# Shorter lead of a max pass, its first products in another order, and exp products on five banks at the end

## The chip, the cores and the metric

One core of a Trainium2 chip runs the whole program. The metric is the device time of one execution in microseconds (us), the median of several runs.

## What is computed

The input is `x` with 2048 tokens of 512 values, in float32, and a conditioning row `c`. A block of attention and a block of MLP follow each other, each behind a layer normalisation whose scale, shift and gate come from `c`:

```python
mod = (_silu(c) @ w_mod).reshape(c.shape[0], 6, 1, -1)
sa, ca, ga, sb, cb, gb = (mod[:, 0], mod[:, 1], mod[:, 2], mod[:, 3], mod[:, 4], mod[:, 5])
h = _layernorm(x, axis=-1) * (1 + ca) + sa
x = x + ga * _A_ref(h, A_wq, A_wk, A_wv, A_wo)   # 32 heads of 16 queries' values, one head of keys and values, softmax
h = _layernorm(x, axis=-1) * (1 + cb) + sb
x = x + gb * _B_ref(h, B_w1, B_b1, B_w2, B_b2)   # gelu(h @ w1 + b1) @ w2 + b2, 1376 hidden values
```

## The kernel before

**Precision.** Products of weights and activations are made from a high and a low part of each operand (names that end in `H` and `L`), three products instead of one. In the scores, the high and low parts of queries and keys lie in different rows of the same operand (`qst`, `ks`), so that one product with 64 rows does it all. Such a product uses half of the rows of TensorE's array (PE); one on the upper half and one on the lower half can run together. The kernel writes the half as `s` (0 or 1). "Whole" products use all 128 rows.

**Units.** The 2048 queries are cut in 8 blocks of 256, and the 32 heads in 8 groups of 4. A pair of them is a unit; there are 64. For every unit two passes run over all 2048 keys.

- The max pass (`Max.step`, L490 to L529): 32 products `m<-ks,qst` (L505) write 128 x 512 scores each to one of three PSUM banks with the tag "m", and DVE reduces each to its row maximum (L510). After a unit's last reduction, `put_max` takes the maximum over the key blocks (`mm`, L558), transposes it (`turned`, L559), and puts off, by `later`, two steps: `gather` (L553, four copies on POOL, then the split in `mh` and `ml`), and `send` (L548, four DMAs that write the maxima into rows 48 and 49 of the unit's `qst`). `MAX_WAIT` holds by how many clocks each is put off.
- The exp pass (`sexp`, from L588): 8 steps of 4 products `e<-qst,ks` (L607), whose rows 48 and 49 subtract the maximum in the same product. ACT makes the exponential of each (L611). The results `p` go into 16 small products with the values, `acc` (L628, `pv`). The `e` products use three banks in turn (`banks`).

A unit's exp pass cannot start before its maxima have landed in `qst`.

**The order.** Each engine works through its list in the order in which the program writes the instructions; no scheduler changes it. The main loop (from L1349) goes through the units in double steps, steps X and Y. A double step has 8 products of `e`, 32 of `acc`, normally 8 products of the max pass of a later unit, and one batch of other products from a queue. `lead` says how far the max pass is ahead: `LEAD` = 6 means 24 products more than the next unit needs. `clock` counts 4 in a double step; `later(n, fn)` has `fn` done n clocks on, when `due()` comes by.

**The queue.** It holds the query projections of later blocks, and for each block, once its attention is done, `rest`: the output projection (`wops`), the second normalisation (`ve`, `rs`, `xh`, on POOL for most blocks), the transposes (`tp`), the first layer of the MLP (`w1ps`) with its gelu, and the second (`w2ps`). `take` gives out a batch of such products, cut by `batches`. In the loop they are issued as halves (`halves`), so that they share the array with products of the scores. `rest` of block b runs beside the attention of block b + 1. What is left of block 6's `w2` products after the loop fills pauses in the tail, where block 7's `rest` runs alone (`tick`, `TAIL`), as whole products.

**The prologue.** `SLOTS` lists in what order key, value and query projections, transposes and other preparations are written, and how many products of the max pass (`chunk`) go between. `FIRST_MAX` is the order of the first products, of units 0 and 1, by key blocks of 512: unit 0 block 0, unit 1 block 0, and so on. Each (unit, block) is 8 products by (twice 4). `low_k` (L400, on DVE) makes the low half of a key block, and `repeat_k` (L404, on ACT) copies it to the other half of the array. `keep_warm(WARM[3])` (L1348) issues five products without use ahead of the first `e`.

**Two lines at the change.** `modl` (L290) are products for the second normalisation's scale and shift, which are put in the prologue by `late_rows`; `qL` is the low part of a query projection, which `send_q` writes to memory (`dq`), from where `load_q` fetches it to `qst`.

Of the kernel before, what the change touches and what calls it, by code (L numbers as in the profile page):

```python
# [18 lines left out]

GELU_R = 0.044715 ** 0.5  # L20

LEAD = 6
LEAD_0 = 6
FIRST_MAX = ((0, 0), (1, 0), (0, 1), (1, 1), (0, 2), (0, 3), (1, 2), (1, 3))
SLOTS = ((2, "keys 1", "keys 1"), (2, "keys 1", "keys 1"), (2, "low 1", "heads 2"), (2, "heads 2", "k 1"), (1, "warm"), (1, "heads 2"), (2, "heads 2", "v 0"),
# [4 lines left out]
MAX_WAIT = (1, 4)  # L30
QBUFS = 4
PREP = 4
BUSY = 5
# [3 lines left out]
TAIL = (4, 8)  # L37
GROUP = 4
NORM_WAIT = 6
WARM = (4, 16, 2, 5)  # L40
MOD_WAIT = 3
AHEAD = 4.5
STIR = ((0, 4, 8, 12), (16, 32, 48, 0))
# [2 lines left out]
def raw(ap):  # L46
    return ap.bitcast(F32)
# [3 lines left out]
def adaln_mqa_mlp(  # L51
# [99 lines left out]
    def due():  # L151
        now = [p for p in pending if p[0] <= clock[0]]
        pending[:] = [p for p in pending if p[0] > clock[0]]
        for _, fn in now:
            fn()
# [11 lines left out]
    def batches(ps, pairs, size, ready=lambda n: True, begin=True, end=True):  # L167

        todo = [(a, b_) for wh, wl, xh, xl in pairs for a, b_ in ((wh, xh), (wl, xh), (wh, xl))]
        last = len(todo) - 1  # L170

        ends = list(range(len(todo), 0, -size))[::-1]
        for begin_, end_ in zip([0] + ends, ends):
            part = range(begin_, end_)
            while not ready(part[-1] // 3):
                yield -1
            yield [(ps, *todo[n], begin and n == 0, end and n == last) for n in part]
# [255 lines left out]
    def qproj(b, g):  # L433

        ps = psum.tile([P, BQ], F32, name=f"qps{b}_{g}", tag="v" if g else "x")
        yield from mm3(ps, qpairs(b, g), 3, 1)
        qH, qL = qtiles(b, g)
        if g == 0:
            nc.scalar.copy(qH, ps)
            nc.vector.tensor_tensor(out=qL, in0=ps, in1=raw(qH), op=ALU.subtract)  # L440
        else:
            q32 = pro.tile([P, BQ], F32, name=f"q32_{b}_{g}", tag="h32", bufs=4)
            nc.scalar.copy(q32, ps)
            split(qH, qL, q32, act, pool)
        send_q(b, g, qH, qL)
        yield -2

# [32 lines left out]
    class Max:  # L480


        def __init__(self):
            def products(u, kcs):
                return [(u, j, t, kc) for kc in kcs for j in range(2) for t in range(blocks[units[u][0]][1] // P)]

            def in_rows(u):
                return [(u, j, t, kc) for j in range(2) for t in range(blocks[units[u][0]][1] // P) for kc in range(NKC)]


            begin = [o for u, kc in FIRST_MAX for o in products(u, [kc])]
            self.todo = [begin + [o for u in range(2, NU) for o in in_rows(u)] for _ in range(2)]
            self.mx, self.left, self.done = {}, list(size), 0

# [34 lines left out]
    def put_max(u, mx):  # L529

        T = blocks[units[u][0]][1] // P
        qst = qsts[u]
        mm = mms[u % 2]
        turned = att.tile([P, 32], F32, name=f"turned{u}", tag="turned", bufs=2)
        if u == 0:
            pad(att, 256, "pad7")
        mt = att.tile([4 * T, P], F32, name=f"mt{u}", tag="mt", bufs=2)
        mh = att.tile([4 * T, P], F32R, name=f"mh{u}", tag="mh", bufs=2)  # L540
        ml = att.tile([4 * T, P], F32R, name=f"ml{u}", tag="ml", bufs=2)

        def send():
            for s in range(2):
                for r, src in ((48, mh), (49, ml)):
                    dst = qst[64 * s + r:64 * s + r + 1].rearrange("p j (t n) -> p (j t) n", n=P)
                    ring = nc.scalar if u == 0 and s else nc.sync
                    ring.dma_start(out=raw(dst), in_=raw(src[2 * T * s:2 * T * (s + 1), :].unsqueeze(1)))  # L548
            placed.add(u)

        def gather():
            for g in range(0, P, 32):
                nc.gpsimd.tensor_scalar(out=mt[:, g:g + 32], in0=turned[g:g + 4 * T, :], scalar1=1.0, scalar2=0.0,  # L553
                                        op0=ALU.mult, op1=ALU.add)
            split(mh, ml, mt, nc.gpsimd, nc.gpsimd)

        def reduce():
            nc.vector.tensor_reduce(out=mm[:, :4 * T], in_=mx, axis=AX.X, op=ALU.max)  # L558
            nc.vector.transpose(out=turned, in_=mm)  # L559
            later(MAX_WAIT[0], gather)  # L560
            later(MAX_WAIT[1], send)


        if NQ <= u < NQ + 2:
            reduce()
        else:
            later((0 - clock[0]) % 4 + 1, reduce)
# [22 lines left out]
    def sexp(u, K, j, s, line=None):  # L590

        w = blocks[units[u][0]][1]
        qst = qsts[u]
        assert u in placed
        n = u * steps[0] + K
        if n < 3 and n not in pbufs:
            pbufs[n] = att.tile([P, 2, 2, 512], F32, name=f"p{n}", tag="p", bufs=3)
        pt = pbufs[n % 3]
        bank = banks.pop(0)
        banks.append(bank)  # L600
        e = psum.tile([P, 512], F32, name=f"e{u}_{K}_{j}_{s}", tag=f"e{bank}", bufs=1)
        rows = slice(64 * s, 64 * s + 64)
        if w == 512:
            kt, rhs = K, qst[rows, j, :]
        else:
            kt, rhs = 2 * K + j, qst[rows].rearrange("p j n -> p (j n)")
        nc.tensor.matmul(e, ks[rows, kt * P:(kt + 1) * P], rhs, start=True, stop=True)  # L607
        dst = pt[:, j, s, :]

        def exp():  # L610
            ins = nc.scalar.activation(dst, e, AF.Exp, scale=0.25)  # L611
            for old in written.pop((n - 3, j, s), ()):
                tc.declare_no_dep(ins.ins, old, reason="the products that read the tile's last contents come between the two")
            written.setdefault((n, j, s), []).append(ins.ins.name)
            return ins

        return exp() if line is None else line.append(exp)
# [190 lines left out]
    def rest_steps(b, fast, rp, bank, ons, ready):  # L808
# [4 lines left out]
        for hf in range(w // HQ):  # L813
# [201 lines left out]
            for t in range(2):  # L1015
                sl = slice(t * P, (t + 1) * P)
                for cols in (slice(0, D), ):
                    place = dict(tag="m", bufs=3) if b == len(blocks) - 2 and t else bank()
                    ps = psum.tile([P, D], F32, name=f"w2ps{b}_{hf}_{t}_{cols.start}", **place)
                    ops = [(gH[:, f, sl], gL[:, f, sl], w2H[:, f, cols], w2L[:, f, cols]) for f in range(NF)]  # L1020
                    size_ = BATCH - 1 if b == len(blocks) - 2 and not t else BATCH
                    yield from batches(ps[:, :cols.stop - cols.start], ops, size_, lambda f: made.issuperset(range(f + 1)))
                    if fast:
                        later(1, lambda t=t, ps=ps, cols=cols: store(t, ps, cols))
                        yield 2
                    else:
                        store(t, ps)
# [126 lines left out]
    def resume():  # L1154

        go_on(holder[0])
# [69 lines left out]
    def q_group():  # L1226
        for i in range(KD):
            next(projections[0])
            if i == KD - 1:
                next(projections.pop(0))  # L1230
            yield

    def warm():
        keep_warm(WARM[2], tag="x")
# [112 lines left out]

    keep_warm(WARM[3], tag="e2", bufs=1)  # L1348
    behind = None  # L1349
    for u in range(NU):  # L1350
        for K in range(0, steps[u], 2):
            goal = lead[u] + (lead[u + 1] - lead[u]) * (K + 2) / steps[u]
# [37 lines left out]

            due()
            batch = take() if behind else None
            short = batch and products(batch) < SHORT + 0.01
            if short:
                issue(mixture(maxes(1, n // 2), exps(1, [(X, 0), (X, 1)])),
                      exps(0, [(X, 0)]) + halves(batch, 0) + [(1.0, lambda: follow(0, X, 1))])
            elif batch:
                groups = [mixture(maxes(1, n // 2, 0.01), beside(1, [(X, 0), (X, 1), (Y, 0)])),  # L1400
                          halves(batch, 0) + [(1.0, lambda: follow(0, X, 0))]]
                issue(*(reversed(groups) if batch[0][3] else groups))
            else:
                plain(1, X, 0, (n + 2) // 4)
# [3 lines left out]
                end_step(*behind)  # L1408
            clock[0] += 1
            due()  # L1410
            if batch:

                reduces, gone = [], []

# [85 lines left out]
```

## Time and profile before

| | |
|---|---|
| median of 3 runs | 1564.13 us |
| the runs | 1564.13, 1564.03, 1564.39 us |
| span of the profiled execution | 1563.1 us, clock 1.000 |
| PE busy | 1546.5 us (99%) |
| DVE busy | 1401.7 us (90%) |
| ACT busy | 1228.8 us (79%) |
| POOL busy | 681.7 us (44%) |

The profiled execution gives its span only, from its first to its last instruction; the timed runs lie about 1 us above it. Rows of the profile name the line, the engine, the operation and output<-input; "x" gives how many. In a row of the timeline the first two numbers are the start and the duration in us, and a bracket at its end says how long the engine was idle before and who ended that. PEld is PE's weight load.

### The profile page before, as it was taken

What the parts mean: (1) busy time and instruction counts of PE and PEld (TensorE: products, weight loads), DVE (VectorE), ACT (ScalarE), POOL (GpSimd) and SP (SyncE); (2) the same over time, 40 slices, a digit from 0 to 9 for tenths busy, and PEclk for the clock granted to TensorE, in tenths of its full rate; (3) what the DMA queues carried; (4) which work ended last, traced back from release to release, by engine and by line L of the source; (5) the groups of instructions that cost most, each with busy time, mean ns of one, the idle gap of its engine ahead of it and who ended that gap; (6) DMA issues with size and microseconds to landing.
All of it is one profiled execution on the core that took longest, in us unless ns stands there. A gap on an engine that the chain in (4) does not pass through costs nothing.

```text
span 1563.1 us, 41433 instructions
## 1 busy us (share of the span) xinstructions
PE 1546.5 (99%) x16387; PEld 959.9 (61%) x16387; DVE 1401.7 (90%) x2479; ACT 1228.8 (79%) x2392; POOL 681.7 (44%) x1194
## 2 busy tenths in 40 slices
PE   7999999999999999999999999999999999999999
PEld 4455555567655665557655675556655676556667
DVE  7999999999999999999999999999999999999625
ACT  5577778788777887788877887788877888788853
POOL 5545433877323570246422472245611573235711
PEclk9999999999999999999999999999999999999999
DMA  7235412313030211213022120303112130312241
GB/s 244 97 96 194 152 52 89 120 52 97 19 110 19 83 60 35 93 29 99 29 62 69 57 84 26 105 16 97 43 50 79 46 97 20 102 34 66 81 150 61
DMA packets 83126, 121.63 MB, mean 78 GB/s; under 512 B 19614, under 2 KB 56222, under 8 KB 82676
## 3 DMA queue, kind: packets, MB, share of 16 engines
q1 hardware_dynamic: 82916, 118.97, 23.5%
q8 instruction: 130, 2.13, 0.6%
q14 instruction: 64, 0.52, 0.1%
q10 hardware_dynamic: 16, 0.00, 0.0%
HBM read 91.13 MB, written 27.27 MB: 76 GB/s over the span
## 4 chain that ended last, share of the span: by engine, by line
PE 84%; DVE 10%; issue 3%; POOL 2%; DMA 1%; ACT 0%; ACTq 0%; SPq 0%; POOLq 0%; DVEq 0%
PE acc L628 28%; PE m L505 24%; PE e L607 16%; DVE mx L510 8%; PE w1ps L191 8%; PE w2ps L181 2%; PE w2ps L191 1%; PE w1ps L181 1%; DMA xt<-in_A_x_dram 1%; PE qps L191 1%; PE tp L191 1%; PE wops L191 1%; PE kps L162 1%; DVE st L835 1%; DVE x L828 1%
## 5 line engine op out<-in xcount | busy, mean ns | idle before, releaser
L510 DVE TENSOR_REDUCE mx<-m 128x1 f32<-128x512 f32 x2048 | 1270.5, 682 | 86.9 <-PE m L505 63.8
L611 ACT ACTIVATE p<-e 128x512 f32<-128x512 f32 x2048 | 1099.3, 598 | 257.4 <-PE e L607 110.5
L505 PE MATMUL m<-ks,qst 64*128 64x512 f32 x2048 | 832.4, 429 | 1.9 <-DVE mx L510 0.6
L607 PE MATMUL e<-qst,ks 64*128 64x512 f32 x2048 | 747.6, 412 | 0.1
L628 PE MATMUL acc<-p,va 128*32 128x256 f32 x8192 | 548.0, 385 | 0.0
L505 PEld LDWEIGHTS m<-ks,qst 64*128 64x128 f32 x2048 | 366.5, 184 | 212.3 <-DVE mx L510 174.8
L607 PEld LDWEIGHTS e<-qst,ks 64*128 64x128 f32 x2048 | 362.5, 184 | 95.2 <-ACT p L611 71.1
L628 PEld LDWEIGHTS acc<-p,va 128*32 128x32 f32 x8192 | 213.7, 109 | 213.1 <-issue 110.0
L553 POOL TENSOR_SCALAR mt<-turned 8x32 f32<-8x32 f32 x256 | 53.1, 208 | 418.9 <-DVE turned L559 406.9
L191 PE MATMUL w1ps<-h2H,w1t 64*128 64x256 f32 x1232 | 235.6, 287 | 0.0
L191 PEld LDWEIGHTS w1ps<-h2H,w1t 64*128 64x128 f32 x1232 | 185.8, 184 | 28.9 <-DVE mx L510 17.7
L191 PE MATMUL w1ps<-h2L,w1t 64*128 64x256 f32 x616 | 169.2, 275 | 0.0
L191 PE MATMUL w2ps<-w2H,gH 64*128 64x512 f32 x284 | 123.8, 436 | 0.0
L191 PEld LDWEIGHTS w1ps<-h2L,w1t 64*128 64x128 f32 x616 | 114.0, 185 | 0.0
L191 PE MATMUL w2ps<-w2L,gH 64*128 64x512 f32 x282 | 110.9, 393 | 0.0
L191 PE MATMUL w2ps<-w2H,gL 64*128 64x512 f32 x282 | 110.2, 391 | 0.0
L954 POOL TENSOR_SCALAR tt<-tt 128x256 f32<-128x256 f32 x77 | 31.0, 403 | 142.6 <-ACT tt L953 109.3
L137 POOL TENSOR_TENSOR gL<-z,gH 128x256 fp32r<-128x256 f32 x77 | 57.0, 740 | 6.4
L955 POOL TENSOR_TENSOR tt<-tt,z 128x256 f32<-128x256 f32 x77 | 56.7, 736 | 6.4
L965 POOL TENSOR_TENSOR z<-tt,z 128x256 f32<-128x256 f32 x77 | 56.4, 733 | 6.0
L964 POOL TENSOR_TENSOR tt<-tt,z 128x256 f32<-128x256 f32 x77 | 56.4, 732 | 0.0
L191 PEld LDWEIGHTS w2ps<-w2H,gL 64*128 64x128 f32 x282 | 52.2, 185 | 0.4
(190 smaller groups left out, 1480.9 us busy)
## 6 DMA issues: line engine op xcount, KB each, us to landing
w1t<-dw SPq DMA_DIRECT2D x82, 512.0 KB
qst<-dq SPq DMA_DIRECT2D x384, 32.0 KB
do<-oc SPq DMA_DIRECT2D x64, 128.0 KB
dw<-w1s SPq DMA_DIRECT2D x11, 512.0 KB
xt<-in_A_x_dram SPq DMA_DIRECT2D x4, 1024.0 KB
dq<-qH SPq DMA_DIRECT2D x16, 256.0 KB
dq<-qL SPq DMA_DIRECT2D x16, 256.0 KB
x<-in_A_x_dram SPq DMA_DIRECT2D x8, 512.0 KB
```

What stands on the lines that cost most here:

```text
L137: eng_l.tensor_tensor(out=dst_l, in0=src, in1=raw(dst_h), op=ALU.subtract)
L181: nc.tensor.matmul(ps, a, b_, start=first_, stop=last_)
L191: ins = nc.tensor.matmul(ps, a[rows], b_[rows], start=first_ and s == 0, stop=last_ and s == 1)
L505: nc.tensor.matmul(m, qsts[u][rows, j, t * P:(t + 1) * P], ks[rows, kc * 512:(kc + 1) * 512], start=True, stop=True)
L510: nc.vector.tensor_reduce(out=self.mx[u][:, i, kc:kc + 1], in_=m, axis=AX.X, op=ALU.max)
L553: nc.gpsimd.tensor_scalar(out=mt[:, g:g + 32], in0=turned[g:g + 4 * T, :], scalar1=1.0, scalar2=0.0, op0=ALU.mult, op1=ALU.add)
L607: nc.tensor.matmul(e, ks[rows, kt * P:(kt + 1) * P], rhs, start=True, stop=True)
L611: ins = nc.scalar.activation(dst, e, AF.Exp, scale=0.25)
L628: ins = nc.tensor.matmul(accs[u][32 * cidx:32 * cidx + 32, :], va[:, kt, :], rhs, start=kt == 0, stop=kt == NKT - 1)
L955: nc.gpsimd.tensor_tensor(out=tt, in0=tt, in1=z, op=ALU.mult)
L964: nc.gpsimd.tensor_tensor(out=tt, in0=tt, in1=z, op=ALU.mult)
L965: nc.gpsimd.tensor_tensor(out=z, in0=tt, in1=z, op=ALU.add)
```

## The change

1. The lead of the max pass falls from 24 to 16 products (`LEAD`, `LEAD_0`). In PE's list in the loop, each max product is one that came a double step earlier in the order of the max pass, and the max pass ends one double step later: 12 instead of 14 steps have none.
2. `FIRST_MAX` puts four products of unit 1's second key block behind unit 0's third and fourth block; unit 0 is complete after 44 products, not 48. `SLOTS` is rearranged: `v 2`, `q 1` and `v 3` come earlier, `rows` (the `modl` products) comes last and behind unit 0's end.
3. In the prologue's query projection, the subtraction for `qL` comes after a pause of its generator, and with it the sends. In `gather` of unit 0, two of the four copies are on ACT.
4. The five products without use ahead of the first `e` go (`WARM`).
5. `send` comes two clocks after the maximum instead of four (`MAX_WAIT`).
6. When no max products are left, two of the banks with the tag "m" join the three of the `e` products. Each step then writes its four `e` products first, alternating between the halves, then half of a batch of `w2` products as whole ones.
7. Block 6's first `w2` tile takes batches of 4 (`SHORT`) instead of 5, and `batches` lets a leading batch of one product join the next. 25 instead of 28 `w2` products of block 6 are done in the loop; the tail has 17 instead of 20 in front of the last `wops` and 24 instead of 18 behind it.

By the lists of the engines, POOL's copies for the units whose number is 3 mod 8 (from 11 on) come behind `ve` and `rs` of the block and ahead of `xh`. The five-bank part and the constants, from the diff:

```diff
-LEAD = 6
-LEAD_0 = 6
-FIRST_MAX = ((0, 0), (1, 0), (0, 1), (1, 1), (0, 2), (0, 3), (1, 2), (1, 3))
+LEAD = 4
+LEAD_0 = 4
+FIRST_MAX = ((0, 0, 4), (1, 0, 4), (0, 1, 4), (1, 1, 2), (0, 2, 4), (0, 3, 4), (1, 1, 2), (1, 2, 4), (1, 3, 4))
...
-         (0, "v 2"), (2, "q 1"), (2, "q 1"), (2, "q 1"),
-         (2, "q 1", "rows"), (2, "v 3", "wq 2"), (2, "rows"), (2, "rows"), (2, "rows", "wq 3", "load"))
-MAX_WAIT = (1, 4)
+         (0, "v 2", "q 1"), (2, "q 1"), (2, "q 1"), (2, "q 1"), (2, "q 1", "v 3"),
+         (2, "rows", "wq 2"), (2, "rows"), (0, "rows"), (0, "rows", "wq 3", "load"))
+MAX_WAIT = (1, 2)
...
-WARM = (4, 16, 2, 5)
+WARM = (4, 16, 2, 0)
...
         ends = list(range(len(todo), 0, -size))[::-1]
+        if ends[0] == 1:
+            ends.pop(0)
...
-            split(qH, qL, q32, act, pool)
+            nc.scalar.copy(qH, q32)
+            yield -2
+            nc.gpsimd.tensor_tensor(out=qL, in0=q32, in1=raw(qH), op=ALU.subtract)
...
-            begin = [o for u, kc in FIRST_MAX for o in products(u, [kc])]
+            parts = {(u, kc): products(u, [kc]) for u in range(2) for kc in range(NKC)}
+            begin = [parts[u, kc].pop(0) for u, kc, n in FIRST_MAX for _ in range(n)]
...
+                if u == 0 and g >= P // 2:
+                    nc.scalar.copy(mt[:, g:g + 32], turned[g:g + 4 * T, :])
+                    continue
...
-        e = psum.tile([P, 512], F32, name=f"e{u}_{K}_{j}_{s}", tag=f"e{bank}", bufs=1)
+        if not isinstance(bank, int):
+            e = bank
+        else:
+            e = psum.tile([P, 512], F32, name=f"e{u}_{K}_{j}_{s}", tag=f"e{bank}", bufs=1)
...
-                    size_ = BATCH - 1 if b == len(blocks) - 2 and not t else BATCH
+                    size_ = SHORT if b == len(blocks) - 2 and not t else BATCH
...
+            if not bare[0] and not mp.has(0) and not mp.has(1):
+                bare[0] = True
+                banks[:0] = [psum.tile([P, 512], F32, name=f"e_{i}", tag="m", bufs=3) for i in range(2)]
+
+            def alone(K, part):
+                issue(exps(0, [(K, 0), (K, 1)]), exps(1, [(K, 0), (K, 1)]))
+                whole(part)
+
             due()
             batch = take() if behind else None
             short = batch and products(batch) < SHORT + 0.01
-            if short:
+            if bare[0]:
+                alone(X, batch[:len(batch) // 2] if batch else [])
+            elif short:
...
-            if batch:
+            if bare[0]:
+                alone(Y, batch[len(batch) // 2:] if batch else [])
+                if batch:
+                    resume()
+                    advance()
+            elif batch:
```

More of the change, by code (lines that the diff above doesn't have):

```diff
@@ L488, in in_rows @@
                 return [(u, j, t, kc) for j in range(2) for t in range(blocks[units[u][0]][1] // P) for kc in range(NKC)]
-            begin = [o for u, kc in FIRST_MAX for o in products(u, [kc])]
+            parts = {(u, kc): products(u, [kc]) for u in range(2) for kc in range(NKC)}
+            begin = [parts[u, kc].pop(0) for u, kc, n in FIRST_MAX for _ in range(n)]
+            assert not any(parts.values())
             self.todo = [begin + [o for u in range(2, NU) for o in in_rows(u)] for _ in range(2)]
@@ L1229, in q_group @@
             if i == KD - 1:
-                next(projections.pop(0))
+                last = projections.pop(0)
+                next(last)
             yield
+        next(last, None)
+        yield
     def warm():
@@ L1349, in adaln_mqa_mlp @@
     behind = None
+    bare = [False]
     for u in range(NU):
```

## The prediction, made before the changed kernel ran

> **What bounds the kernel now.** I read the page first: the span, the engines' shares, the chain that ended last and the costliest groups.
>
> ```profile
> span 1563.1 us, 41433 instructions
> PE 1546.5 (99%) x16387; PEld 959.9 (61%) x16387; DVE 1401.7 (90%) x2479; ACT 1228.8 (79%) x2392; POOL 681.7 (44%) x1194
> PE 84%; DVE 10%; issue 3%; POOL 2%; DMA 1%; ACT 0%; ACTq 0%; SPq 0%; POOLq 0%; DVEq 0%
> L510 DVE TENSOR_REDUCE mx<-m 128x1 f32<-128x512 f32 x2048 | 1270.5, 682 | 86.9 <-PE m L505 63.8
> ...
> L607 PE MATMUL e<-qst,ks 64*128 64x512 f32 x2048 | 747.6, 412 | 0.1
> ```
>
> PE is busy 99% of the span and holds 84% of the chain. DVE, with its 2048 reductions of the max pass, comes next. In front of its 2048 exp products PE lost 0.1 us in all (last column): every unit's maxima were in place in time. The profiled execution's span is 1563.1 us; the timed runs (median 1564.13) lie 1.0 above it, and I add that 1.0 to every sum. Then the windows, by stage: one block of the main loop, and the stretch near its end in which no max products are left.
>
> ```profile
> 297.00:477.00 180.00, 179.90 (x2017) 112.50 (x2012) 168.67 (x295) 147.49 (x289) 88.61 (x153) 1.00 0.22 67
> 1478.00:1510.00 32.00, 32.00 (x312) 18.17 (x311) 1.76 (x2) 26.76 (x52) 10.93 (x19) 1.00 0.24 84
> ```
>
> The columns are the window, its length, then busy time of PE, PE's weight loads, DVE, ACT and POOL, the granted clock (1.00), and the DMA share. In a block PE works 179.90 of 180.00 us. So from the first exp product to the end of the loop every us that goes must be a us of PE work, and every wait that is added in front of a PE instruction is paid whole. Only three places are not like this: the prologue, the stretch without max products, and the tail. The change touches all three. As written out per engine, PE's list inside the loop stays the same, except that each max product there is one that came eight places (one double step) earlier in the max pass's order.
>
> **The prologue: about 1.5 us earlier.** The loop's first exp products wait for unit 0's maximum. The chain of waits and the engines' timeline:
>
> ```profile
> 71.61 0.93 ACTq L548
> ...
> 72.63 2.18 DMA qst<-ml
> ...
> 74.85 0.56 PE e L607 x2
> ```
>
> ```profile
> 53.64 0.68 DVE L400 TENSOR_TENSOR ks<-kps,ks 16x512 fp32r<-16x512 f32 x1
> 54.35 0.62 ACT L404 CAST ks<-ks 16x512 fp32r<-16x512 f32 x1 [0.75 <-DVE ks L400]
> 59.66 0.68 DVE L400 TENSOR_TENSOR ks<-kps,ks 16x512 fp32r<-16x512 f32 x1
> 60.38 5.22 DVE L510 TENSOR_REDUCE mx<-m 128x1 f32<-128x512 f32 x8
> 66.63 2.48 DVE L510 TENSOR_REDUCE mx<-m 128x1 f32<-128x512 f32 x4 [1.03 <-PE m L505]
> 69.67 1.02 POOL L553 TENSOR_SCALAR mt<-turned 8x32 f32<-8x32 f32 x4 [0.33 <-DVE turned L559]
> 73.35 1.42 PE L285 MATMUL idle<-wkH 128*128 128x512 f32 x5
> ```
>
> Unit 0's maximum ends with the reduction that is over at 69.11 (66.63 + 2.48), the 48th. The new order puts four products of unit 1's second key block behind it, so it is the 44th: 4 x 0.65 (5.22 / 8) = 2.6 us less. Against it stands that DVE no longer has those reductions to do while a key block's low half is made and copied. In the old list the subtraction at 53.64 was followed by reductions that need nothing new; now unit 0's products of block 2 come at once, and they need the copy of 54.35 (to 54.97) and a product before DVE can go on. A reduction could begin at about 55.5 (54.97 and a product of 0.5), where one began at 54.35: 1.1 lost. At block 3 (59.66) the pattern is the same, but the products moved behind block 2 cover about half of it: 0.5, an estimate. So 2.6 - 1.6 = 1.0. The gather of the maxima, four copies of 0.26 on POOL, now has two on ACT: 0.5. The five idle products that go (1.42 us at 73.35) ended before the rows landed at 74.81, so they cost nothing now. The first exp product then starts at about 73.3 instead of 74.85. Bounds: 0 if the waits eat all of it; 3.1 (2.6 + 0.5) if there are none. The value is nearer the middle, -1.5.
>
> **The steps without max products: about -3.3 us.** These are the starts of the accumulation (`acc`) in the chain of waits; one step lies between two of them.
>
> ```profile
> 1468.44 1.00 PE acc L628 x16
> ...
> 1471.28 1.00 PE acc L628 x16
> ...
> 1474.08 1.00 PE acc L628 x16
> ...
> 1476.88 1.00 PE acc L628 x16
> ...
> 1508.32 1.86 PE acc L628 x32
> ```
>
> A step with max products takes 2.84 (1471.28 - 1468.44); the two without them that still have `w1` halves take 2.80; the twelve with `w2` halves take 31.44 / 12 = 2.62. PE's list after the change has max products in the former two (2 x 0.04 = +0.1) and the new form in all twelve: four exp products alternating between the array's halves, then two (once three) whole `w2` products, then `acc`. What such groups cost is seen where half and whole products follow each other in the prologue:
>
> ```profile
> 62.45 0.50 PE L505 MATMUL m<-ks,qst 64*128 64x512 f32 x2
> 62.87 0.50 PE L162 MATMUL qps<-h0H,wqH 128*128 128x512 f32 x1
> 63.22 0.39 PE L162 MATMUL qps<-h0H,wqL 128*128 128x512 f32 x1
> 63.45 0.40 PE L162 MATMUL qps<-h0L,wqH 128*128 128x512 f32 x1
> 63.77 0.50 PE L505 MATMUL m<-ks,qst 64*128 64x512 f32 x2
> ```
>
> A pair of halves to the first whole product is 0.42, the next starts are 0.35 and 0.23 apart, and 0.32 goes to the next pair: a group of k takes 0.23 k + 0.2. So a new step is 1.00 (`acc`) + (2 x 0.23 + 0.2) + (2 x 0.23 + 0.2) = 2.32, against 2.62: 12 x 0.30 = 3.6, less 0.23 for the third product, 3.3. ACT does not take over: four exps in a row take 2.06 (next row), 1.96 from start to start, under 2.32; with three banks it stands idle 0.3 a step, with five it need not.
>
> ```profile
> 1478.35 2.06 ACT L611 ACTIVATE p<-e 128x512 f32<-128x512 f32 x4
> ```
>
> That the exp products pair up is as good as shown: the two `m` halves at 62.45 took one slot and the change (0.42), not two slots. Bounds: 0 if waits for banks eat the difference; -5.9 if changing between halves and whole costs nothing (2.12 a step).
>
> **The tail: +1.4 us.** The shorter batches leave more of block 6's `w2` products for behind the loop: 17 instead of 20 in front of the last `wops`, 24 instead of 18 behind it.
>
> ```profile
> 1514.55 4.59 PE w2ps L181 x20
> 1519.14 1.89 PE wops L181 x6
> 1521.04 4.13 PE w2ps L181 x18
> 1525.17 0.44 PE tp L912 x4
> ```
>
> ```profile
> 1518.68 0.41 ACT L132 CAST onH<-os_last 128x256 fp32r<-128x256 f32 x1 [8.05 <-DVE os_last L666]
> 1525.02 0.55 DVE L847 TENSOR_SCALAR xh<-x,mv,rs 128x512 f32<-128x512 f32 x1 [0.46 <-POOL rs L844]
> ```
>
> The last `wops` starts at 1519.14 because `onH` is cast until 1519.09, so three products fewer ahead of it leave PE idle and gain nothing. Behind it the transposes `tp` started as the filling ended, with the normalised rows nearly there; six more products are 6 x 0.229 (4.13 / 18) = +1.4 on the path.
>
> **The shorter lead: 0 as I take it.** Each unit's maximum is now ready one double step (5.6 us) less ahead of its first exp product. Where nothing stands in between, the sends come two clocks, half a double step (2.8), earlier behind the gather than before, so those units lose only the other half, and I take it that each of them had that much in hand, since none was late before (0.1 us). The tight ones are the seven whose number is 3 mod 8 (11 to 59): POOL's copies for them now stand behind the normalisation's two small operations, and the sends wait for that.
>
> ```profile
> 672.61 0.24 POOL L842 TENSOR_SCALAR ve<-mv 128x2 f32<-128x2 f32 x1 [4.41 <-DVE mv L841]
> 672.93 0.72 POOL L844 TENSOR_TENSOR rs<-ve,mhalf 128x2 f32<-128x2 f32 x1
> 673.76 4.14 POOL L847 TENSOR_SCALAR xh<-x,mv,rs 128x512 f32<-128x512 f32 x2
> 678.97 0.29 PEld L607 LDWEIGHTS e<-qst,ks 64*128 64x128 f32 x2
> ```
>
> ```profile
> 1469.91 0.33 SPq L646 DMA_DIRECT2D do<-oc  x1
> 1471.60 0.58 SPq L705 DMA_DIRECT2D sums<-do  x1
> ```
>
> In unit 27 `rs` ends at 673.65. Four copies, the cast and the subtraction as in unit 0 (1.02 + 0.06 + 0.3 + 0.5) and four issues bring the last issue to about 677.2; the exp product needs the row at 678.97, 1.77 later. The nearest rows are 1.69 (on SP's queue, from the issue of `do` at 1469.91 to its reader at 1471.60) and 2.18 (unit 0's `ml`, on ACT's queue). These sends are on SP's queue, so I take 1.69: in time, 0. At 2.18 each is 0.41 late, 7 x 0.41 = +2.9. `xh` itself moves behind the copies by 1.9 us, to the moment at which the transposes need it: 0. Unit 63's copies now stand behind the last gelu operations; being one unit, it is small beside the seven.
>
> [...]
>
> **Sum.** -1.5 - 3.3 + 0.1 + 1.4 + 0 = -3.3: a span of 1559.8, a time of 1560.8 us.
>
> **Rivals.** First, *the rows come late* (slower). Same place, the seven units above: if the last issue and the landing together pass the 1.77 us by a stall s, the time is 1560.8 + 7 s. It decides at s = 0.92, a landing of 2.7 us, and beyond that cancels and outruns the gain: s = 0.92 gives 1567.3, s = 1.1 gives 1568.5. For it: SP's line also carries the weight loads, and behind these a send can wait; no slack remains to take it. Against: the same queue shows 1.69. With the 2.18 of the other queue it is 1563.7, no change. Second, *the new steps gain nothing* (2.62 stays, because four exp products in a row meet banks that ACT has not emptied yet, or because the changes between halves and whole cost more than in the prologue): 1560.8 + 3.3 = 1564.1, no change. Against: ACT's 1.96. Third, *the prologue gains nothing*, the waits for the key blocks take the place of the four reductions: 1562.3, no change by itself. Fourth, *more gain*: no loss in changing between halves and whole, 2.12 a step, 1558.2. For it: within a group the products already start 0.23 apart. Against: the 0.42 and 0.35 above.
>
> **How the numbers follow.** 0.2% (3.1 us) is about what a measurement of this kernel can tell from no change, so faster starts below 1561.0, and my forecast lies just beyond that line. Chances: the forecast, give or take 1.2, 0.50, of which 0.33 is below the line; more gain 0.13; late rows 0.22, of which 0.15 is far enough to be slower; no gain in the steps or the prologue 0.15, which is no change. Faster 0.46, same 0.17 + 0.07 + 0.15 = 0.39, slower 0.15. The range reaches down to 1557.4 (more gain, and half of what the prologue may still give), up to 1565.6 (neither gain, with the +1.5 of tail and steps left); outside lie the late rows that make it slower, 0.15, and 0.05 below.
>
> **What would show it.** Right: the first exp product near 73.3; `acc` of the last twelve steps 2.3 apart, with ACT nearly without idle time; the last transposes about 1.4 later behind the end of the loop; in blocks, 180 us as before. Wrong: exp products whose idle time ends with the rows `qst<-ml` in units 11 to 59; `acc` starts 2.6 apart; a first exp product at 74.8.

## The result: slower by 0.6%, and the profile after

The changed kernel takes 1573.50 us (median of 5 runs, 1571.87 to 1575.34) against 1564.14 us before (5 runs, 1564.03 to 1565.55): the ratio is 1.0057, with a 95% interval of 1.0046 to 1.0068. The forecast was 1560.8 us, with a range up to 1565.6. PE's granted clock, as a share of full speed, is 1.000 in the trace of the kernel before; beside the experiments that kernel was timed 60 times more, at 0.999 or 1.000 in all but four (0.997 and 0.998, 1567.1 to 1568.5 us). The changed kernel's runs have 0.994 to 0.998, and the longer ones have the lower clocks on the whole.

From the page of the changed kernel (span; busy time; exp products with PE's idle time in front of them in the last column):

```profile
span 1570.3 us, 41358 instructions
PE 1546.9 (99%) x16354; PEld 957.0 (61%) x16354; DVE 1400.9 (89%) x2479; ACT 1229.7 (78%) x2394; POOL 681.2 (43%) x1192
L619 PE MATMUL e<-qst,ks 64*128 64x512 f32 x2048 | 742.7, 412 | 5.4 <-DMA qst<-ml 5.4
```

PE waits 5.4 us for the rows of maxima, where it waited 0.1. Where, tells the list of waits, over the whole span and from 297 to 480 us alone (us in total, times, longest):

```profile
PE e L619 <- DMA qst<-ml: 5.4, 3, 4.2
...
PE e L619 <- DMA qst<-ml: 4.5, 2, 4.2
```

Most of it is one wait of 4.2 us, at unit 12. The clock shows in the windows; it changes at 64.56, 67.98, 344.46 and 351.28, the ends of the rows with 0.50 (window, length, busy time of PE, PE's weight loads, DVE, ACT, POOL, then the clock, 0.50 for half speed):

```profile
57.74:61.15 3.41, 3.41 (x16) 1.69 (x15) 3.33 (x6) 1.56 (x3) 0.00 (x0) 1.00 0.02 5
61.15:64.56 3.41, 2.36 (x9) 1.10 (x8) 2.16 (x4) 1.01 (x3) 0.00 (x0) 1.00 0.00 0
64.56:67.98 3.42, 3.42 (x10) 1.84 (x8) 2.40 (x4) 0.00 (x0) 0.00 (x0) 0.50 0.00 0
...
341.04:344.46 3.42, 1.64 (x20) 0.60 (x18) 2.43 (x5) 1.36 (x4) 2.98 (x9) 1.00 0.01 3
344.46:351.28 6.82, 4.41 (x34) 3.26 (x34) 2.08 (x3) 2.28 (x4) 0.27 (x1) 0.50 0.13 33
```

Twice PE worked at half clock: for 3.4 us in the prologue, behind a window in which it was busy 2.36 of 3.41 us, and for 6.8 us at unit 12, behind one with 1.64 of 3.42. In the second stretch PE worked 4.41 us at half speed, so it lost about 2.2, an estimate (4.41 / 2). In the kernel before, the window of this length around the same place of the prologue held 3.13 us of PE work:

```profile
59.12:62.53 3.41, 3.13 (x11) 1.52 (x11) 3.29 (x6) 1.34 (x3) 0.00 (x0) 1.00 0.00 0
```

PE's list holds the exp products in the same order in both kernels, so their starts can be compared one by one. Read from the two timelines:

| | before | after | later by | added since the row above |
|---|---|---|---|---|
| first of unit 0 | 74.85 | 75.23 | 0.38 | 0.38 |
| first of unit 12 | 341.22 | 346.88 | 5.66 | 5.28: the wait (4.34) and 0.94 in units 9 to 11 |
| first of unit 13 | 364.02 | 371.85 | 7.83 | 2.17: half clock |
| first of unit 59 | 1399.17 | 1408.35 | 9.18 | 1.35: 0.3 at a time |
| start of the last `acc` | 1508.32 | 1514.46 | 6.14 | -3.04: the steps without max products |
| end of the span | 1563.1 | 1570.3 | 7.2 | 1.06: the tail |

The steps at the end did what was forecast. In the chain of waits:

```profile
1486.14 1.00 PE acc L640 x16
...
1488.53 1.00 PE acc L640 x16
...
1512.14 1.00 PE acc L640 x16
...
1514.46 1.88 PE acc L640 x32
...
1520.71 3.91 PE w2ps L183 x17
...
1524.64 1.89 PE wops L183 x6
1526.53 5.51 PE w2ps L183 x24
1532.04 0.44 PE tp L924 x4
```

From 1486.14 to 1514.46 there are twelve steps, 28.32 us, 2.36 each.

Why unit 12 waits is seen on POOL's and SP's timelines. Its maxima are turned on DVE, then copied by POOL (`mt`), then sent:

```profile
334.49 0.21 DVE L568 STREAM_TRANSPOSE turned<-mm 128x32 f32<-128x32 f32 x1
334.97 1.28 POOL L1144 TENSOR_TENSOR w2f<-w2f,gb 128x512 f32<-128x512 f32 x1
...
338.29 1.29 POOL L1144 TENSOR_TENSOR w2f<-w2f,gb 128x512 f32<-128x512 f32 x1
...
341.63 1.02 POOL L562 TENSOR_SCALAR mt<-turned 8x32 f32<-8x32 f32 x4
...
345.10 0.57 SPq L554 DMA_DIRECT2D qst<-ml  x1
...
346.88 0.76 PE L619 MATMUL e<-qst,ks 64*128 64x512 f32 x1 [4.20 <-DMA qst<-ml]
```

And before:

```profile
327.74 0.21 DVE L559 STREAM_TRANSPOSE turned<-mm 128x32 f32<-128x32 f32 x1
...
328.23 1.02 POOL L553 TENSOR_SCALAR mt<-turned 8x32 f32<-8x32 f32 x4
...
333.80 1.28 POOL L1132 TENSOR_TENSOR w2f<-w2f,gb 128x512 f32<-128x512 f32 x1
```

The last two pieces of `w2`, scaled and split on POOL (334.97 to 341.67 after), stood behind unit 12's copies before; with the shorter lead they stand ahead of them. `turned` is ready at 334.70 and waits 6.9 us.

### The profile page after: what moved, and what is told of

Same layout as the page of the kernel before. It is cut to its first block, busy times and chain, and to the rows that moved or that the text cites. A ratio compares the mean times of both kernels' runs of the same rounds, so it can differ in the third digit from the quotient of the medians.

```text
span 1570.3 us, 41358 instructions
## 1 busy us (share of the span) xinstructions
PE 1546.9 (99%) x16354; PEld 957.0 (61%) x16354; DVE 1400.9 (89%) x2479; ACT 1229.7 (78%) x2394; POOL 681.2 (43%) x1192
## 4 chain that ended last, share of the span: by engine, by line
PE 91%; DVE 5%; DMA 1%; POOL 1%; ACT 1%; issue 0%; SPq 0%; DVEq 0%; POOLq 0%
PE acc L640 31%; PE m L511 26%; PE e L619 17%; PE w1ps L193 8%; DVE mx L516 4%; PE w2ps L183 2%; PE w2ps L193 2%; PE qps L193 1%; PE wops L193 1%; PE w1ps L183 1%; DMA xt<-in_A_x_dram 1%; PE tp L193 1%; PE kps L162 1%; PE wops L183 0%; DMA qst<-ml 0%; PE tp L375 0%
## 5 line engine op out<-in xcount | busy, mean ns | idle before, releaser
L193 PE MATMUL w2ps<-w2H,gH 64*128 64x512 f32 x264 | 115.8, 439 | 0.0
L193 PE MATMUL w2ps<-w2L,gH 64*128 64x512 f32 x264 | 103.5, 392 | 0.0
L193 PE MATMUL w2ps<-w2H,gL 64*128 64x512 f32 x264 | 103.0, 390 | 0.0
L976 POOL TENSOR_TENSOR tt<-tt,z 128x256 f32<-128x256 f32 x77 | 56.5, 733 | 0.0
```

The lines of the kernel that those rows point to most:

```text
L193: ins = nc.tensor.matmul(ps, a[rows], b_[rows], start=first_ and s == 0, stop=last_ and s == 1)
L976: nc.gpsimd.tensor_tensor(out=tt, in0=tt, in1=z, op=ALU.mult)
```

## The experiments

Theory 1: the loss is one place on POOL's list, and the pauses of PE that it and the new prologue make bring the clock to half. Theory 2: the rows land late through SP's line or the DMAs. Theory 3: the loss is spread over the units.

**The weight pieces put aside.** In the changed kernel, no weights are prepared while unit 11 runs.

```diff
-            if clock[0] >= prepared[0] + PREP and weights and weights[0] in preps and not state["busy"]:
+            if clock[0] >= prepared[0] + PREP and weights and weights[0] in preps and not state["busy"] and u != 11:
```

> The changed kernel, but the last two pieces of w2 are not prepared while unit 11 runs, so POOL has the gather of unit 12 ahead of them in its list. Theory 1 (the loss is one place: unit 12's copies stand behind 6.7 us of weight preparation on POOL, its first exp product waits 4.2 us, and in that pause the clock gate falls to half for 6.8 us): the wait of unit 12 goes, and 4.2 + about 2.2 us with it, against the changed kernel's 1573.5: 1566 to 1567.5, and the mean clock rises to 0.999 (one half-speed stretch of 3.4 us in the prologue left). Theory 2 (the rows land late because SP's line or the DMAs are slow, wherever POOL has the copies): unit 12 is as late as before, 1572 to 1575.

Measured: 1571.95 us (1570.64 to 1576.73), ratio to before 1.0053 (1.0041 to 1.0066). Unit 12's rows were in time, so theory 2 falls; the time did not follow. The two pieces now stand between the steps of the gelu on POOL, and ACT waits for these with its exponentials queued behind:

```profile
350.88 1.28 POOL L1144 TENSOR_TENSOR w2f<-w2f,gb 128x512 f32<-128x512 f32 x1
...
354.96 0.72 POOL L977 TENSOR_TENSOR z<-tt,z 128x256 f32<-128x256 f32 x1
355.72 0.42 ACT L965 ACTIVATE tt<-z 128x256 f32<-128x256 f32 x1 [4.05 <-POOL z L977]
...
356.67 0.79 PE L619 MATMUL e<-qst,ks 64*128 64x512 f32 x1 [3.51 <-ACT p L623]
```

A wait of 3.5 us for a free bank took the place of the 4.2, and behind it the clock was at half for 6.8 us again (355.51 to 362.34; 16 `acc` products took 1.94 us at 357.40, 1.07 at 350.49): 6.3 us are lost between the first products of units 12 and 13, where the changed kernel loses 6.5 around unit 12. In this run the prologue kept its full clock, and the first exp product came at 73.28.

**Unit 12's wait filled.**

```diff
+            if (u, K) == (12, 0):
+                ps = psum.tile([P, 512], F32, name="fill12", tag=f"e{banks[0]}", bufs=1)
+                for _ in range(18):
+                    nc.tensor.matmul(ps, ks[:, 0:P], ks[:, 0:512], start=True, stop=True)
```

> The changed kernel with 18 products without use (18 x 0.23 = 4.1 us) put in PE's list in front of unit 12's first exp product, so that PE works through the wait; nothing is done to the wait itself. If the clock falls because PE is idle (theory 1), it stays at 1 there: first exp product of unit 12 at the same 346.9, but 2.2 us less behind it: 1570 to 1572. If the clock falls for another reason (the load of the chip, the phase of something free-running), nothing changes: 1572 to 1575.

Measured: 1577.14 us (1571.66 to 1578.22), ratio 1.0071 (1.0058 to 1.0083). The median is worse than that of the changed kernel; in the profiled run (clock 0.995) the prologue, which is unchanged, had 17 us at half clock (first exp product at 79.53), and the runs' clocks go from 0.992 to 1.000. So the time decides nothing here. At unit 12, where the test is, the windows show full clock, through the filled wait (first row) and behind it:

```profile
347.64:351.05 3.41, 3.41 (x17) 2.58 (x15) 0.00 (x0) 0.00 (x0) 1.38 (x3) 1.00 0.01 2
351.05:354.46 3.41, 3.41 (x42) 2.44 (x42) 2.49 (x5) 2.52 (x6) 0.00 (x0) 1.00 0.14 41
```

Unit 12 is 4.3 us later again, and between units 12 and 16 only 0.15 more is lost, where it was 2.1. So in this trace the half clock there went when PE no longer stood idle, with the wait itself still in place.

**The prologue filled, first try.**

```diff
+            "fill 2": one(lambda: keep_warm(3, tag="e0", bufs=1)), "fill 3": one(lambda: keep_warm(3, tag="e1", bufs=1)),
```

(`fill 2` stands behind the first `keys 3` in `SLOTS`, `fill 3` behind the first `q 1`.)

> The changed kernel with three products without use ahead of unit 0's first product on key block 2, and three ahead of that on block 3, where PE waits 0.9 us each for the keys' low half. If these pauses bring the clock down to half at 64.6 us (for 3.4 us), it stays at 1 now, DVE gets its products sooner, and the first exp product comes 1.0 to 1.7 us earlier than 75.2; the time falls by as much, to about 1572. If the clock has another cause, the first exp product stays at 75.2 or comes a little later, and the time is that of the changed kernel.

Measured: 1580.32 us (1575.52 to 1581.73), ratio 1.0092 (1.0079 to 1.0105). The bank was one that ACT still had to read, so the filling itself waited, and the pause grew to 1.78 us. Timeline, then windows:

```profile
56.44 0.97 PE L287 MATMUL idle<-wkH 128*128 128x512 f32 x3 [1.78 <-ACT va L415]
```

```profile
54.85:58.26 3.41, 1.82 (x7) 1.12 (x8) 1.04 (x2) 1.55 (x4) 1.50 (x3) 1.00 0.00 0
58.26:82.15 23.89, 23.05 (x66) 10.30 (x68) 13.46 (x23) 4.77 (x12) 2.57 (x7) 0.50 0.02 7
```

Behind the longer pause came a longer stretch at half clock, 23.9 us, and the five runs, at clocks of 0.990 to 0.997, are all slower than those of the changed kernel. Against its intention, this speaks for the pauses. That the pause alone sets the length is not shown: the run before this one had 17 us with the pauses of the changed kernel.

**The same on a free bank** (both with `tag="e2"`).

> As the filled prologue before it (three products without use ahead of unit 0's products on key blocks 2 and 3), but written to a PSUM bank that nothing holds, so that they don't wait themselves: in the first try they waited for a copy out of their bank and made the pause longer (1.78 us), and the clock was at half for 23.9 us. If pauses of PE bring the clock down, now no stretch of half speed should be left before the first exp product in any run: it comes at 73.0 to 73.6, the loss of unit 12 (4.3 and 1.6 to 2.2) stays, and the time is 1570 to 1572 with a spread of under 2 us. If pauses don't matter, the prologue's half-speed stretches come and go as before, and the runs spread by 4 us and more.

Measured: 1571.97 us (1570.73 to 1572.48), ratio 1.0046 (1.0034 to 1.0058), spread 1.8 us. No half clock ahead of the loop; the windows that were short of work are now 3.07 busy:

```profile
53.57:56.98 3.41, 3.07 (x11) 1.54 (x9) 2.65 (x5) 2.22 (x6) 1.48 (x2) 1.00 0.00 0
60.40:63.81 3.41, 3.07 (x12) 1.83 (x11) 2.74 (x5) 1.93 (x4) 0.00 (x0) 1.00 0.02 5
```

The first exp product comes at 73.94, not the 73.0 to 73.6 expected, 0.7 to 1.0 us later than in the two traces that kept full clock without the filling (72.98 and 73.28). What is left over the kernel before is unit 12 and the small losses.

**The lead back in the loop alone** (`LEAD = 6`, `LEAD_0 = 4`).

> The changed kernel with LEAD = 6 again (LEAD_0 stays 4, so the prologue is the same and the lead grows by 8 products over units 0 to 7). Theory 1: from unit 8 on the gather of unit 12 has its old place ahead of the weight preparation, so the wait goes with its half-speed stretch (-6.4), and with it the small losses of 0.3 in front of the units 3 mod 8 (-1.9); against it 8 more products in the first eight units, which cost DVE or PE up to 1: 1564.5 to 1566.5. Theory 3 (the loss is spread over all units by the new steps and sends): under 2 us of it goes, 1571 or more.

Measured: 1569.77 us (1566.75 to 1576.18), ratio 1.0037 (1.0022 to 1.0052); higher than expected. In the profiled run (1566.75, clock 1.000) unit 12's copies are at 332.14, ahead of both weight pieces, as before, and PE waits for rows 0.2 us in all:

```profile
332.14 1.01 POOL L562 TENSOR_SCALAR mt<-turned 8x32 f32<-8x32 f32 x4
337.73 1.28 POOL L1144 TENSOR_TENSOR w2f<-w2f,gb 128x512 f32<-128x512 f32 x1
```

```profile
PE e L619 <- DMA qst<-ml: 0.2, 1, 0.2
```

From unit 12 to unit 56 it loses nothing against the kernel before. But making up the eight products over units 0 to 7 costs 5.8 us (from 1.9 earlier at unit 0 to 3.9 later at unit 12), not 1. The other runs, up to 1576, have clocks of 0.993 to 0.999; where the clock fell in them no trace shows.

**Unit 12's copies on ACT and DVE.**

```diff
+        def gather12():
+            for g in range(0, P, 32):
+                nc.scalar.copy(mt[:, g:g + 32], turned[g:g + 4 * T, :])
+            split(mh, ml, mt, nc.scalar, nc.vector)
...
-            later(MAX_WAIT[0], gather)
+            later(MAX_WAIT[0], gather12 if u == 12 else gather)
```

> The changed kernel, but unit 12's maxima are copied by ACT (four copies and the high part) and DVE (the low part), not by POOL; nothing else is moved, and the weight preparation stays where it is on POOL. If POOL's line is what makes unit 12 late, its wait of 4.3 us and the half-speed stretch behind it go, and nothing comes in their place: 6 us less than the changed kernel, span 1562 to 1564 where the prologue keeps full clock, mean clock 0.998 to 1.0. If SP or the landing is to blame, the wait stays at 3 us or more.

Measured: 1570.46 us (1568.57 to 1573.77), ratio 1.0044 (1.0031 to 1.0057). Unit 12's last rows are sent 7.6 us ahead of its first exp product (339.82 and 347.38), and PE no longer waits for them, with POOL's weights where they were. In place of that wait DVE, with the low part in its line, waits for ACT 1.4 us, and PE then for DVE:

```profile
337.82 0.28 DVE L137 TENSOR_TENSOR ml<-mt,mh 8x128 fp32r<-8x128 f32 x1 [1.41 <-ACT mh L132]
...
338.76 0.54 PE L511 MATMUL m<-ks,qst 64*128 64x512 f32 x1 [1.63 <-DVE mx L516]
```

That pause too was followed by half clock: PE was busy 1.78 us from 335.68 to 339.09, and the clock was at half from there to 342.50 (16 `acc` products took 1.93 us at 339.23, 1.07 at 343.32). Of the 6.5 us that the changed kernel loses around unit 12, 3.1 are left. So POOL's line was the cause of the wait for rows, and "nothing comes in its place" was wrong.

**`LEAD = LEAD_0 = 6`.**

> The changed kernel with LEAD = LEAD_0 = 6. Eight more products of the max pass stand ahead of the first exp product; DVE has some 2.6 us to spare for them while unit 0's rows travel, so the first exp product comes at 73.5 to 75.5 instead of 73.0. In the loop nothing is late any more (no wait in unit 12, no 0.3 before the units 3 mod 8), and the steps at the end gain 3.1 to 3.7 as in the changed kernel, less 0.7 to 1.0 in the tail. Span 1559.5 to 1561.5 at full clock, against 1563.1 of the kernel before: 0.1 to 0.2% faster, if the prologue's pauses don't bring the clock down; each half-speed stretch of 3.4 us there adds up to 1.7.

Measured: 1570.18 us (1566.31 to 1574.58), ratio 1.0037 (1.0023 to 1.0050): slower than before, not faster. In the profiled run (clock 0.997) the first exp product came at 78.51, with half clock from 56.5 to 59.9 and from 80.4 to 87.2. Behind unit 4 nothing more is lost, so unit 12 is in time with the earlier sends (`MAX_WAIT`) of the changed kernel: its wait belongs to the lead.

**The same, with the two pauses filled** (two products each, on `e2`).

> The changed kernel with LEAD = LEAD_0 = 6 and two products without use, on a free bank, in front of unit 0's products on key blocks 2 and 3. With LEAD = 6 alone the runs went from 1566 to 1575, with clocks from 0.991 to 0.998; with the pauses filled the clock stays at 1 in nearly every run, and the spread shrinks to under 2 us. At full clock: first exp product 74 to 75.5, no wait in unit 12, end steps as in the changed kernel: 1561 to 1563.5. If the pauses were not the cause of the half-speed stretches, runs of 1566 and more remain.

Measured: 1566.63 us (1565.14 to 1568.06), ratio 1.0011 (1.0002 to 1.0020). The spread fell from 8.3 to 2.9 us, all runs at 0.997 or 0.998. That is 3 us over the expectation, and eight of the 11 runs are at 1566 or more, which the expectation had put down to a cause other than the pauses. The trace shows one stretch of half clock left, where PE waits for DVE between single max products, in front of the first exp product (76.02):

```profile
73.78:77.20 3.42, 3.01 (x11) 1.42 (x10) 3.42 (x7) 0.67 (x2) 1.51 (x3) 1.00 0.20 48
77.20:84.02 6.82, 6.82 (x35) 3.74 (x36) 5.70 (x10) 3.79 (x8) 0.00 (x0) 0.50 0.02 5
```

**That place filled too** (`keep_warm(2, tag="e2", bufs=1)` behind each of the eight products).

> As the run before (LEAD = LEAD_0 = 6, two products without use ahead of key blocks 2 and 3; 1566.6 us, one stretch of 6.8 us at half clock from 77.2 us on in its trace), with two more products without use behind each of the eight max products that stand ahead of the first exp product, where PE waits for DVE between them. If PE's pauses bring the clock down, that stretch goes too: first exp product at 76.0 to 76.6, 1.5 to 2.5 us less, 1564 to 1565.2, and clocks of 0.999 to 1.0 in the runs. If it is the start of the exp products itself that brings the clock down, nothing changes: 1566.5 and 0.998.

Measured: 1569.85 us (1569.37 to 1570.50), ratio 1.0035 (1.0021 to 1.0048). The clock stays at full speed to the end of the loop in the profiled run, and the runs are at 0.999 or 1.000 with a spread of 1.1 us. The price is far over the estimate: max product and filling now take turns every 1.09 us where DVE did 16 reductions in 9.65 us, 0.60 each, in the run before, and the first exp product is 5 us later, at 81.06.

**The new steps alone.** The kernel before with parts 6 and 7 of the change.

> The kernel before with parts 6 and 7 of the change alone (five banks and whole products once no max products are left, shorter batches, so more for the tail). By the prediction's step: 12 steps x 0.30 - 0.23 = 3.3 less, two steps with w1 in the new form on top (0 to 0.6 less), 0.7 to 1.4 more in the tail: 2 to 3 us faster than before, at full clock throughout. If the new steps gained only because the shorter lead had changed what stands beside them, it is within 1 us of before.

Measured: 1562.39 us (11 runs, 1561.48 to 1562.70), ratio 0.9983 (0.9975 to 0.9992). The steps are those of the changed kernel, twelve in 28.16 us:

```profile
1476.79 1.00 PE acc L633 x16
...
1502.63 1.00 PE acc L633 x16
...
1504.95 1.92 PE acc L633 x32
```

So they don't need the shorter lead, and are worth 2.3 us, tail included (1564.67 - 1562.39).

**The lead alone.** The kernel before with `LEAD = 4` and `MAX_WAIT = (1, 2)`.

> The kernel before with LEAD = 4 (LEAD_0 stays 6) and MAX_WAIT = (1, 2), and nothing else: the prologue is that of the kernel before, and from unit 8 on the lead is that of the changed kernel. POOL's list has unit 12's gather behind the last two pieces of w2 again. If the loss in unit 12 belongs to the lead alone, it is there with the same size: 4.3 us of wait and 1.6 to 2.5 behind it at half clock, then 0.3 in each unit 2 mod 8; the eight products of lead given up spare up to 1 to 3 us over units 0 to 7, and cost as much where the max pass ends. Together 6 to 9 us slower than before, 1571 to 1574. If the prologue's part was needed for the loss (a different phase at unit 12), under 3 us slower.

Measured: 1574.47 us (1573.36 to 1575.26), ratio 1.0060 (1.0048 to 1.0073): 9.7 us slower than before, a little over the 6 to 9 expected. The loss is there, with the prologue of the kernel before: the wait, and the half clock behind it.

```profile
340.90 1.02 POOL L553 TENSOR_SCALAR mt<-turned 8x32 f32<-8x32 f32 x4
```

```profile
346.14 0.55 PE L607 MATMUL e<-qst,ks 64*128 64x512 f32 x1 [4.21 <-DMA qst<-ml]
```

```profile
346.40:349.80 3.40, 3.40 (x26) 2.59 (x28) 2.01 (x3) 1.86 (x4) 0.00 (x0) 0.50 0.19 48
```

**A version that is faster than both.** Parts 6 and 7 on the kernel before, with unit 0's gather split between POOL and ACT and `WARM` ending in 3.

> The kernel before with parts 6 and 7 (the one before this ran 2.3 us faster with them) and, of part 3, the split of unit 0's gather between POOL and ACT, with three instead of five products without use ahead of the first exp product so that these end before it. The prologue keeps its order, with its windows of 3.4 us at least 0.92 busy. The first exp product comes 0.5 earlier, 74.3 to 74.5, and the time is 1561.5 to 1562.2, 0.2% under the kernel before, at full clock in every run. If the shorter filling lets the clock fall, some runs are 1.7 us longer.

Measured: 1561.64 us (11 runs, 1560.60 to 1564.09), ratio 0.9980 (0.9971 to 0.9989): 0.2% faster than the kernel before. All runs are at clocks of 0.999 or 1.000 but one (0.998, 1564.09 us), so "full clock in every run" did not hold; the kernel before had two such runs among 21 beside it. Beyond the 2.3 us of the new steps, the split gather is not shown to bring anything: the intervals of the two kernels overlap, and in this run's trace the first exp product was at 75.34. In kernels with the prologue of the kernel before it lay between 74.49 and 75.43 in single traces, so half a us can't be read from it.

## Why the prediction was wrong, point by point

**The shorter lead, "0 as I take it": this step failed.** It took it that in all units but the seven 3 mod 8 nothing stands between the maxima and the sends, and that each then has the lost 2.8 us in hand; beyond the 0.1 us of waiting before, it had no row for either. The second was right for unit 12: before, its last rows were sent at 331.69, 9.5 us ahead of its first exp product at 341.22. The first was wrong: in the first block's turn POOL has 6.7 us of weight preparation to do, and the change moves unit 12's copies behind it, which the term held as 0 and which cost 4.3 us of waiting. The rival "the rows come late" named the mechanism, and its condition was a wait for landed rows, but put it at seven places by 1 us; it was one place by 4.3.

For the seven units the landing was in time: the three waits for rows in the list (0.9 at unit 0, 0.3 at unit 10, 4.2 at unit 12) are none of them. The reading of 1.77 us from the last issue to the exp product held, with 1.75 to 1.78 in units 11 to 51 and 1.48 in unit 59. But unit 12's exp product, which did wait for its rows, came 1.78 behind the last issue, so these units may have nothing to spare. No trace shows how much they have in hand, and that it was enough is in part luck.

What those blocks do lose, 0.3 a block from 2 mod 8 on, is DVE's: two small instructions for the maximum (`mm`, `turned`) now stand in a stretch where DVE holds the chain. From the last block statistics (`st`) to the next reductions it took 0.57 us before and takes 0.89 after. Before, then after:

```profile
671.87 0.42 DVE L835 BATCH_NORM_STATS2 st<-x 128x6 f32<-128x256 f32 x1
672.20 0.33 DVE L841 BATCH_NORM_AGGREGATE mv<-st 128x2 f32<-128x12 f32 x2
672.44 3.03 DVE L510 TENSOR_REDUCE mx<-m 128x1 f32<-128x512 f32 x5
```

```profile
679.88 0.41 DVE L847 BATCH_NORM_STATS2 st<-x 128x6 f32<-128x256 f32 x1
680.21 0.17 DVE L567 TENSOR_REDUCE mm<-mx 128x8 f32<-128x32 f32 x1
680.48 0.21 DVE L568 STREAM_TRANSPOSE turned<-mm 128x32 f32<-128x32 f32 x1
...
680.77 3.02 DVE L516 TENSOR_REDUCE mx<-m 128x1 f32<-128x512 f32 x5
```

**The sum took the clock as 1.00 throughout.** That was read from the trace of before and carried over to a kernel with more pauses; no term and no rival held it. At unit 12 the half clock cost 2.2 us of the profiled run. In the prologue it ate the gain.

**The prologue, -1.5 us: right in size, at full clock.** In two traces of the same prologue without half clock the first exp product came at 72.98 and 73.28, forecast was 73.3. With half clock it came at 75.23 (3.4 us of it) up to 84.11 (23.9 us, with the longer pauses of the first filling). The waits that I counted for DVE were PE's pauses as well, 0.9 us each, and I did not ask what a pause does to PE.

```profile
PE m L511 <- DVE ks L402: 1.8, 2, 0.9
```

**The steps without max products, -3.3 us: right.** 28.32 us instead of 31.44, -3.1; a step 2.36, forecast 2.32. (The bound of 2.12 a step "if changing costs nothing" takes away only one of the two changes of 0.2; without both it would be 1.92. The rival with more gain and the lower end of the range hang on it; no run came near either.)

**The tail, +1.4 us: right behind the last `wops`, 1.1 in sum.** From the last `wops` to `tp` it took 7.40 instead of 6.03 us, +1.37. But the last `wops` came 0.64 earlier (10.18 instead of 10.82 behind the start of the last `acc`), since a DMA that its operand waits for, `os_last<-dr`, landed sooner: the reader on DVE began 3.38 us behind the issue (1520.34 to 1523.72), before 4.03 (1514.18 to 1518.21). What made these 0.65 us the two traces do not show. The span's end is another 0.3 later. From the start of the last `acc` to the end it is 55.6 to 57.9 us in the twelve traces with this tail, and 54.9 and 55.4 in two with the old one: 1.3 apart in the mean. (Runs lie 1.7 to 2.0 us above their own spans, not 1.0, in both kernels: 1572.21 over 1570.3 after. That shifts no difference.)

The forecast itself was -3.3; +4.3 for the wait, +2.2 for the half clock behind it, +2.3 for small losses in units 9 to 11 and 13 to 59, +1.9 in the prologue, and -0.2 in steps and tail make the profiled run's +7.2. Of the 0.94 in units 9 to 11, 0.3 is the wait for rows at unit 10; what the rest waits for stays open. The median of the runs is higher still, with lower clocks than this run's.

## What to carry to other kernels

Here the shorter lead was paid for at one unit, 12, whose copies came to stand behind 6.7 us of other work on POOL: go through each engine's list for every unit, not through a typical one. A rearrangement that lets the bounding engine pause can cost more than the pause. Behind a pause of 1.78 us PE spent 23.9 us at half clock, behind two of 0.9 us 3.4 us, so look at the clock behind every pause that a change adds. Fill a pause only with work that has nothing to wait for: the first filling waited for its bank, and the pause grew from 0.9 to 1.78 us. Work that is moved out of the way of one chain must be shown a place where no other chain needs it: twice here a wait went and another took its place (4.2 us for rows, then 3.5 for a bank or 1.6 for DVE).

## What the runs showed of the hardware

At half clock PE stayed 3.42 and 6.82 us in the changed kernel's trace, 3.40 in that of the lead alone, 6.82 in that of `LEAD = LEAD_0 = 6` with two pauses filled, and 23.89 in that of the prologue's first filling. In the 3.4 us ahead of these stretches, at full clock, PE was busy 2.36, 1.64, 0.26, 3.01 and 1.82 us: it had pauses ahead of each, in the fourth case between single products that waited for DVE.

Busy time alone does not tell where the clock falls. From 27.02 to 30.43 in the changed kernel's trace PE was busy 2.53 of 3.41 us, less than the 3.01 of 3.42, and in the 3.41 us behind it the clock was 1.00. Nor did the long stretch end when PE had work again: PE was busy 23.05 of its 23.89 us.

Where the pauses were filled with products that did not wait themselves, single traces show 1.00 in their place: at unit 12 with PE busy 3.41 of 3.41 us, in the prologue with 3.07 of 3.41. But the same prologue, with its pauses, had 3.4 us at half clock in the changed kernel's trace and none in the two whose first exp products came at 72.98 and 73.28. What else decides this no run shows, nor how much of the spread comes from it (3.5 us in the changed kernel's runs, 1.8 with the prologue's pauses filled).
